# Even and odd heads in one PSUM bank each, first decay products straight from PSUM, three low weight parts on TensorE, and a new order for the first pairs

## The chip, the cores and the metric

The kernel runs on one NeuronCore of a Trainium2 chip. Its time is the device time of one execution in microseconds (us). Engines: TensorE (PE; its weight loads are listed as PEld), VectorE (DVE), ScalarE (ACT), GpSimd (POOL) and SyncE (SP, which issues the DMAs).

## The reference

Three stages follow each other: a linear attention with per-channel decay, a gated expert with RMS norm, and a second expert with squared ReLU. There are 4 batches, 8 heads, 768 steps and 48 channels a head; all in float32.

```python
for t in range(S):                      # _attn_ref, state of 48 x 48 per head
    cur = np.einsum('bhd,bhe->bhde', u[None] * kt, vt)
    y[:, :, t] = np.einsum('bhd,bhde->bhe', rt, state + cur)
    state = wt[:, :, :, None] * state + np.einsum('bhd,bhe->bhde', kt, vt)
# _moe_ref, 3072 tokens x 384, d_ff 1536
xn = x / np.sqrt(np.mean(x * x, -1, keepdims=True) + 1e-06) * rms_g
x = (silu(xn @ w_gate) * (xn @ w_val)) @ w_out
# _moe2_ref, d_ff 2048
r = np.maximum(x @ w_in, 0.0)
out = (s * (r * r) + b) @ w_out
```

## The kernel before

**Tiling.** The 768 steps are cut into 6 chunks of 128. A chunk of one batch is a *pair*, numbered jb = 4 * chunk + batch, so there are 24 (jb0 to jb23). Four pairs make the 512 tokens of one chunk that the first expert reads. The first expert has 12 weight blocks f (gate, value and output part of 128 columns each), the second 16.

**Precision.** Every large product is made of three matmuls: high weight by high input, high by low, low by high. Weights arrive as 64-bit words. DVE puts 32-bit floats together from them in three steps (L585, L589, L591), ACT rounds the high part (L595), DVE takes the low part as a difference (L597).

**One pair of attention** (`attention`, L314). DVE scans the decays forward and backward (L335, L342) and multiplies r and k by them. PE makes the scores in two banks (`scores`, L381) and, in the same step, turns k (L390). ACT copies the two banks to a tiles; POOL zeroes one triangle (`affine_select`, L408). PE then makes in one step (`sums`, L440) the part of the old state (L430), the scores by v (L438) and the new state's product (`news`, L449). DVE adds the two result banks and the diagonal term av to ys, and the state's product to ST. ACT squares ys, POOL takes the root (pow), ACT scales to xg, PE flips xg (`flip`, L547) and ACT and DVE write its high and low part (xh, xl) for the expert. jb0 to jb3 are simpler: no old state, the scores by v in one bank (L447), the mask by DVE, the diagonal through `ac` (L393) and `more` (L465).

**Buffers that tie pairs together.** From jb4 on, three PSUM banks (5, 6, 7) go round: a pair takes two for scores, one for turned k, two for sums, one for the state, one for the flip. IN[q], the tile of r and k, has q = jb % 2, so the r and k of jb10 are loaded once jb8's are used up.

**Order.** Nothing is issued in the order in which it is written. Class `Plan` collects every operation with a priority `when` (smaller goes first), the engines that can do it and a cost for each, and then builds one fixed order per engine: whenever an engine is free it gives it the ready operation of smallest `when`. Until the first product of 512 columns is issued, an idle PE gets *fill* matmuls (L803). The first expert runs in parts: chunk 0 with f 0 to 5, chunk 1 with f 0 to 5 (most of both in 256-token halves), chunk 0 with f 6 to 11, chunk 1 with f 6 to 11, then chunks 2 to 5 with all f. In traces and orders the products into the expert are L623 (w_93 is the gate weight of f 6), those out of it L606 to L608. A weight tile is called by a number, as w_91; tiles of f 10 and 11 are w_1679 to w_1683 in the order of before and w_1586 to w_1591 in that of after.

Of the kernel before, what the change touches and what calls it, by code (L numbers as in the profile page):

```python
# [10 lines left out]
F32 = mybir.dt.float32  # L11
# [12 lines left out]
C = 128  # L24
# [26 lines left out]
TD, LATE = 3, 60  # L51
ORDER = -200, -190, -170, -160, -180, -150
TURNED, EARLY, NU, NM, NZ, LENT = 12, 12, 4, 4, 8, 6

# [45 lines left out]
class Plan:  # L100
# [90 lines left out]
def act(n):  # L191
    return 0.10 + 0.825e-3 * n

# [10 lines left out]
def body(ctx: ExitStack, tc: tile.TileContext, rkw, nat, w1, w2, cst, out):  # L204
# [40 lines left out]
    FL, = tiles(1, "fl", [1, 1], I32)  # L245
    PS = [ps.tile([128, NB], F32, name=f"b{i}") for i in range(8)]
    ident = cs[:, CI:CH]
    mask = MK.rearrange("p (o t) -> p o t", o=1).to_broadcast([128, HP, C])
# [39 lines left out]
    def dma(when, dst, src, nbytes, reads=(), writes=(), land=0.0):  # L288
        op(when, {"sp": max(0.47, nbytes / 350e3 + 0.06)}, lambda e: nc.sync.dma_start(
            out=dst, in_=src), reads, writes, land)  # L290
# [23 lines left out]
    def attention(jb, t):  # L314
        q, b = jb % 2, jb % B
        ke, re, ne = (DVE, DVE, DVE) if jb < EARLY else (BOTH, BOTH, BOTH)
        last = jb >= NJ - B
# [47 lines left out]
        if jb >= NU:  # L365
            tt(td, ne, DM, n[0], n[0], n[1], ALU.mult, (), [nk])
            tt(td, ne, DM, n[0], n[0], cs[:, CU:CEND].rearrange("p (h d) -> p h d", h=H), ALU.mult, ["cu"], [nk])
            op(td, {"dve": vec2(DM)}, lambda e: nc.vector.tensor_reduce(
                AC[q].rearrange("p h o -> p (h o)"), n[0], AX.X, ALU.add), [nk], [("ac", q)], False)
            if jb < NZ:  # L370
                def scaled(e):
                    for h in range(H):
                        nc.scalar.activation(AV[q][:, h], v[:, h], AF.Copy, scale=AC[q][:, h])

                op(td, {"act": 8 * act(D)}, scaled, [("ac", q), ("v", q)], [("av", q)])
            else:
                tt(td, DVE if jb < EARLY else BOTH, DM, AV[q], v, AC[q].to_broadcast([128, H, D]), ALU.mult,
                   [("ac", q), ("v", q)], [("av", q)])

        def scores(e):  # L380
            for h in range(HP):  # L381
                for c0 in (0, 64) if jb >= NM else (0,):
                    cols = slice(c0, c0 + 64 if jb >= NM else C)
                    for p in range(2):
# [28 lines left out]
        if jb < NU:  # L413
            def times(e):
                nc.scalar.activation(AC[q].rearrange("p h o -> p (h o)"), up, AF.Copy)
                for h in range(H):
                    nc.scalar.activation(AV[q][:, h], v[:, h], AF.Copy, scale=AC[q][:, h])

            op(t, {"act": 9 * act(D)}, times, [("ps", i), ("v", q)], [("av", q), ("ac", q)])
        iy = [bank(jb) for _ in range(1 + (jb >= B))]  # L420
        i = iy[0]
        Y = [PS[i][:, 0:DM].rearrange("p (h d) -> p h d", h=H) for i in iy]
# [3 lines left out]
        def quarters(e):  # L426
            for h in range(HP):
                for c0 in (0, 64):
                    for p in range(2):
                        nc.tensor.matmul(Y[p][c0:c0 + 64, 2 * h + p, :], r[64 * p:64 * p + D, h, c0:c0 + 64],  # L430
                                         ST[b][64 * p:64 * p + D, h, p, :], start=h == 0, stop=False,
                                         skip_group_check=True)
# [8 lines left out]
        def sums(e):  # L441
            if jb >= B:
                quarters(e)
            else:
                for j in range(H):
                    p, h = divmod(j, HP)
                    nc.tensor.matmul(Y[0][:, 2 * h + p, :], AT[A[p]][:, h, :], v[:, 2 * h + p, :],  # L447
                                     start=j == 0, stop=j == H - 1, skip_group_check=True)
            if U is not None and jb >= NU:  # L449
                news(e)  # L450
# [18 lines left out]
        reads = [("a", s) for s in A]  # L469
        if jb < NU:  # L470
            op(t, {"pe": 1.8}, sums, reads + [("v", q)], [("ps", i)])
            op(t, {"pe": 0.7}, more, [("av", q), "cs"], [("ps", i)])
            op(t, {"pe": 0.6}, news, [("v", q)] + tk, [("ps", iu)])
            ys, yk = PS[i][:, 0:DM], ("ps", i)
        else:
            op(t, {"pe": 1.5 + 0.6 * (not last)}, sums,
               reads + [("r", q), ("v", q), ("st", b, 0), ("st", b, 1)] + tk * (not last),
               [("ps", i) for i in iy] + ([] if last else [("ps", iu)]))
# [9 lines left out]
        if not last:  # L488
            for p, z in ((0, slice(0, 64)), (1, slice(64, RW))):
                s, pmb = ST[b][z, :, p], PM[q][z].to_broadcast([z.stop - z.start, HP, D])  # L490
                if jb >= B:
                    tt(t, ("dve",), HP * D, s, U[z], s, ALU.add, [("ps", iu)], [("st", b, p)])
                    tt(t, BOTH, HP * D, s, s, pmb, ALU.mult, [("pm", q)], [("st", b, p)])
                else:
# [41 lines left out]
    def hand_over(t):  # L536
        op(t, {"pool": 0.0}, lambda e: None, (), ROOM, False)

    def attention_x(jb, t):
        x, b, z = jb // B % 2, jb % B, jb % 2 if jb < NZ else 0  # L540
# [9 lines left out]

        op(t, {"pe": 0.42}, flip, [("xg", z), "cs"], [("ps", i)])
        sl = slice(b * C, (b + 1) * C)
# [9 lines left out]
    def weights(ph, f, t, slots, clamp=False):  # L562
        src = (w1, w2)[ph]
        for c0, n in ((0, 2), (2, 1))[:2 - ph]:
# [28 lines left out]
            for i in range(n):  # L593
                c, s = slice(i * DM, (i + 1) * DM), slots[c0 + i]
                op(t, {"act": act(DM)}, lambda e, c=c, s=s, pat=pat: nc.scalar.activation(  # L595
                    W[s][:, 0], pat(c).bitcast(F32), AF.Copy), [("pat", pi)], [("wh", s)])
                op(t, {"dve": vec2(DM)} if ph == 0 else {"dve": vec2(DM), "pool": gps(DM)}, lambda e, c=c, s=s, pat=pat: E[e].tensor_tensor(  # L597
                    W[s][:, 1], pat(c).bitcast(F32), W[s][:, 0].bitcast(F32), ALU.subtract),
# [177 lines left out]
    def start():  # L776
# [19 lines left out]

        def empty(e):
            for g in ST:
                nc.gpsimd.memset(g.rearrange("p h j d -> p (h j d)"), 0.0)

        def idle():
# [7 lines left out]

        op(-300, {"dve": 1.9}, consts, (), ["c", "z"])  # L810
        op(-300, {"pool": 1.0}, zeros, (), [("g", 0), ("g", 1)], False)
# [205 lines left out]
```

## Time and profile before

| | us |
|---|---|
| median of 3 runs (lowest, highest) | 984.51 (983.59, 984.66) |
| profiled execution | 986.03 |
| its span | 983.5 |
| PE busy | 962.5 (98%) |
| DVE busy | 661.3 (67%) |
| ACT, POOL busy | 370.9, 174.4 |
| share of PE in the chain that ended last | 84% (DVE 8%, DMA 4%) |

PE is busy nearly throughout, so what PE does not do in time, or does in more time, is the run's time. The first 150 us, in which four pairs are made ready and all weights of the first expert are decoded, differ from the rest: DVE is busy there for 136.7 of 150 us and PE stands still or runs fills in places. The granted TensorE clock is full (2.4 GHz) except at the start and in one place at 100 us.

### The profile page before, as it was taken

Reading aid. Unit: us, or ns where it says so; the run is one execution under the profiler, and the core shown is the slowest. Engines: PE = TensorE matmul, PEld = TensorE weight load, DVE = VectorE, ACT = ScalarE, POOL = GpSimd, SP = SyncE. Lnnn points to the kernel's source line nnn. Section 1 sums busy time; section 2 is a strip of 40 time slices with the busy share of each in tenths; the row PEclk is TensorE's granted clock in tenths of the full one; section 3 lists DMA queues with packets and bytes.
Section 4 is the critical chain, followed back from the end, with each engine's and each line's share of the span. In section 5 each row is a group of like instructions: output and inputs, shape, how many; then the busy total and the mean of one; then the engine's idle time right before and its main releaser. Section 6 shows DMA issues by size and latency. Waiting matters only on the chain.

```text
span 983.5 us, 17703 instructions
## 1 busy us (share of the span) xinstructions
PE 962.5 (98%) x7172; PEld 794.9 (81%) x7174; DVE 661.3 (67%) x1080; ACT 370.9 (38%) x751; POOL 174.4 (18%) x232
## 2 busy tenths in 40 slices
PE   9997999999999999999999999999999999999997
PEld 5886888888878888888888878888888888888886
DVE  7998899556655665543388889986778884433332
ACT  4645553343322422333243344343343433433333
POOL 3203210244424234211005440000000000000000
PEclk9999899999999999999999999999999999999999
DMA  7654463233634543222365565553354430000001
GB/s 249 186 161 135 140 192 112 74 112 87 166 91 97 140 115 81 80 71 70 78 221 188 180 202 183 174 170 97 123 182 157 163 130 1 33 1 1 33 1 36
DMA packets 74426, 115.87 MB, mean 118 GB/s; under 512 B 28384, under 2 KB 48096, under 8 KB 74336
## 3 DMA queue, kind: packets, MB, share of 16 engines
q1 hardware_dynamic: 74336, 114.65, 38.5%
q8 instruction: 58, 0.95, 0.4%
q14 instruction: 32, 0.26, 0.1%
HBM read 99.16 MB, written 15.47 MB: 117 GB/s over the span
## 4 chain that ended last, share of the span: by engine, by line
PE 84%; DVE 8%; DMA 4%; ACT 2%; issue 1%; POOL 1%; SPq 0%; DVEq 0%; POOLq 0%; ACTq 0%
PE b L623 45%; PE b L606 11%; PE b L607 11%; PE b L608 11%; DMA raw<-in_w 2%; PE b L438 2%; PE b L386 2%; DVE pat L589 1%; DVE pat L591 1%; PE b L430 1%; DMA in<-in_rkw 1%; DVE eb L342 1%; DVE w L597 1%; DMA n<-in_nat 1%; DVE pat L585 1%
## 5 line engine op out<-in xcount | busy, mean ns | idle before, releaser
L623 PE MATMUL b<-xh,w 128*128 128x512 f32 (+1 forms) x1566 | 487.2, 376 | 1.0 <-DVE sg L295 0.6
L623 PEld LDWEIGHTS b<-xh,w 128*128 128x128 f32 x1566 | 288.2, 189 | 57.3 <-DVE sg L295 2.1
L623 PE MATMUL b<-xl,w 128*128 128x512 f32 (+1 forms) x783 | 291.9, 373 | 0.0
L606 PE MATMUL b<-hh,w 128*128 128x512 f32 (+1 forms) x537 | 205.4, 382 | 1.3 <-ACT in L658 0.7
L607 PE MATMUL b<-hl,w 128*128 128x512 f32 (+1 forms) x537 | 203.2, 378 | 2.0 <-DVE hl L295 2.0
L608 PE MATMUL b<-hh,w 128*128 128x512 f32 (+1 forms) x537 | 202.5, 377 | 0.0
L298 ACT ACTIVATE sg<-b 128x512 f32<-128x512 f32 (+1 forms) x179 | 102.1, 570 | 244.3 <-PE b L623 238.5
L623 PEld LDWEIGHTS b<-xl,w 128*128 128x128 f32 x783 | 147.9, 189 | 25.2
L694 DVE SCALAR_TENSOR_TENSOR sg<-sg,cs,b 128x512 f32<-128x512 f32 (+1 forms) x97 | 71.8, 740 | 88.3 <-ACT sg L298 88.1
L607 PEld LDWEIGHTS b<-hl,w 128*128 128x128 f32 x537 | 101.4, 189 | 20.9 <-DVE hl L295 2.8
L606 PEld LDWEIGHTS b<-hh,w 128*128 128x128 f32 x537 | 101.4, 189 | 20.9 <-ACT in L658 0.9
L608 PEld LDWEIGHTS b<-hh,w 128*128 128x128 f32 x537 | 101.3, 189 | 18.6
L697 DVE SCALAR_TENSOR_TENSOR hl<-sg,cs,hh 128x512 fp32r<-128x512 f32 (+1 forms) x97 | 73.0, 752 | 45.7 <-ACT hh L298 45.6
L298 ACT ACTIVATE hh<-sg 128x512 fp32r<-128x512 f32 (+1 forms) x82 | 47.4, 578 | 136.9 <-DVE sg L295 136.8
L298 ACT ACTIVATE hh<-sg,cs 128x512 fp32r<-128x512 f32 (+1 forms) x97 | 69.8, 720 | 76.5 <-DVE sg L694 73.2
L295 DVE TENSOR_TENSOR sg<-b,sg 128x512 f32<-128x512 f32 (+1 forms) x82 | 50.8, 620 | 60.7 <-PE b L623 60.2
L295 DVE TENSOR_TENSOR hl<-sg,hh 128x512 fp32r<-128x512 f32 (+1 forms) x82 | 57.8, 704 | 21.6 <-ACT hh L298 21.1
L597 POOL TENSOR_TENSOR w<-pat,w 128x384 fp32r<-128x384 f32 x29 | 39.8, 1391 | 67.6 <-ACT w L595 67.6
L408 POOL TENSOR_SCALAR_AFFINE_SELECT a<-a 128x512 f32<-128x512 f32 x38 | 31.4, 846 | 87.5 <-ACT a L298 87.4
L595 ACT ACTIVATE w<-pat 128x384 fp32r<-128x384 f32 x68 | 32.9, 519 | 32.0 <-DVE pat L591 31.9
L295 DVE TENSOR_TENSOR in<-in,eb 112x512 f32<-112x512 f32 x28 | 20.4, 738 | 24.6 <-DMA in<-in_rkw 24.6
L295 POOL TENSOR_TENSOR st<-st,pm 64x192 f32<-64x192 f32 (+1 forms) x38 | 23.1, 607 | 71.9 <-DVE st L295 52.3
(131 smaller groups left out, 876.0 us busy)
## 6 DMA issues: line engine op xcount, KB each, us to landing
raw<-in_w SPq DMA_DIRECT2D x56, 768.0 KB, 4.3
in<-in_rkw SPq DMA_DIRECT2D x24, 448.0 KB, 4.6
raw<-in_w SPq DMA_DIRECT2D x24, 384.0 KB, 3.3
n<-in_nat SPq DMA_DIRECT2D x18, 384.0 KB, 3.4
in<-in_rkw SPq DMA_DIRECT2D x24, 226.6 KB, 3.1
x2d<-o SPq DMA_DIRECT2D x21, 256.0 KB, 2.8
a<-in_rkw SPq DMA_DIRECT2D x24, 224.0 KB, 3.8
v<-in_nat SPq DMA_DIRECT2D x24, 192.0 KB, 4.0
```

The source lines that it names most:

```text
L295: op(when, {e: cost[e] for e in engines}, lambda e: E[e].tensor_tensor(dst, a, b, f), reads, writes, port)
L298: op(when, {"act": act(n)}, lambda e: nc.scalar.activation(dst, src, func, **kw), reads, writes)
L386: nc.tensor.matmul(sc[p][cols, h, c0:], k[rows, h, cols], r[rows, h, c0:], start=True, stop=True, skip_group_check=True)
L408: op(t, {"pool": 0.60}, lambda e, s=A[p]: nc.gpsimd.affine_select(out=AT[s], in_=AT[s], compare_op=ALU.is_gt, fill=0.0, base=0, pattern=[[ ...
L595: op(t, {"act": act(DM)}, lambda e, c=c, s=s, pat=pat: nc.scalar.activation(W[s][:, 0], pat(c).bitcast(F32), AF.Copy), [("pat", pi)], [("w ...
L597: op(t, {"dve": vec2(DM)} if ph == 0 else {"dve": vec2(DM), "pool": gps(DM)}, lambda e, c=c, s=s, pat=pat: E[e].tensor_tensor(W[s][:, 1], ...
L606: nc.tensor.matmul(dst, wt[:, 0, cols], xh, start=first, stop=False, skip_group_check=True)
L607: nc.tensor.matmul(dst, wt[:, 0, cols], xl, start=False, stop=False, skip_group_check=True)
L608: nc.tensor.matmul(dst, wt[:, 1, cols], xh, start=False, stop=last, skip_group_check=True)
L623: nc.tensor.matmul(dst, W[s][:, w, kk * 128:(kk + 1) * 128], xx[x][:, kk, sl], start=first and j == kk == 0, stop=last and kk == KD - 1 an ...
L694: op(t, {"dve": vec2(n)}, lambda e: nc.vector.scalar_tensor_tensor(sg, sg, s_col, p, ALU.mult, ALU.mult), [("ps", i)], [("sg", q)], False)
L697: op(t, {"dve": vec2(n)}, lambda e: nc.vector.scalar_tensor_tensor(hl, sg, b_col, hh.bitcast(F32), ALU.add, ALU.subtract), [("sg", q), ("h ...
```

## The change

- **Sums by head parity.** In `attention` the scores by v use all 128 rows at once: even heads are summed in one bank and odd heads in the other, 16 products of 128 rows by 64 columns in place of 32 of 64 by 64. The two DVE additions that follow take 192 columns each (before: 384 each). The state tile loses its dimension of parity, so its addition and its decay product are one operation of 112 partitions each, not two.
- **First decay products.** For jb0 to jb3, DVE multiplies the new state in PSUM by the decay at once; before, ACT copied it in two operations and DVE or POOL multiplied the copies later. POOL no longer clears ST at the start.
- **Low parts on PE.** For f 0, the three low weight parts are made on PE: identity by float minus identity by high part, in bank 1; ACT copies the result.
- **Diagonal term.** av comes from ACT in four operations of two heads for all jb below 12 (before: ACT below 8, DVE for 8 to 11).
- **Order.** A table FIRST_OPS replaces the priority of about 130 of the first 812 operations, and some costs in the planner are new. The table is cut to two lines here. Operations 747, 751 and 761 in it are a scan, a product and the scores of jb8.

```diff
+FIRST_OPS = {
...
+    511: -263.4, 548: 827.8, 549: 709, 552: 454, 556: 831.9, 590: 439.1, 592: 673.5, 596: 450.7, 605: 467.4,
...
+    685: -155.7, 688: 8.6, 747: 1340.2, 751: 1405.6, 754: 1892.3, 755: -1192.9, 756: -460, 761: 834.5, 800: -206.5,
...
+}
+ONPE = 1
...
-        self.ops.append((when, engines, fn, port))
+        self.ops.append((FIRST_OPS.get(i, when), engines, fn, port))
...
 def act(n):
-    return 0.10 + 0.825e-3 * n
+    return 0.19 + 0.65e-3 * n
...
-    ST = tiles(B, "st", [RW, HP, 2, D])
+    ST = tiles(B, "st", [RW, HP, D])
...
-            if jb < NZ:
-                def scaled(e):
...
-                op(td, {"act": 8 * act(D)}, scaled, [("ac", q), ("v", q)], [("av", q)])
+            if jb < EARLY:
+                scale_v(td, q, v)
             else:
-                tt(td, DVE if jb < EARLY else BOTH, DM, AV[q], v, AC[q].to_broadcast([128, H, D]), ALU.mult,
-                   [("ac", q), ("v", q)], [("av", q)])
+                tt(td, BOTH, DM, AV[q], v, AC[q].to_broadcast([128, H, D]), ALU.mult,
+                   [("ac", q), ("v", q)], AVK)
...
-                        nc.tensor.matmul(Y[p][c0:c0 + 64, 2 * h + p, :], r[64 * p:64 * p + D, h, c0:c0 + 64],
-                                         ST[b][64 * p:64 * p + D, h, p, :], start=h == 0, stop=False,
...
+                        rows = slice(64 * p, 64 * p + D)
+                        nc.tensor.matmul(Y[p][c0:c0 + 64, 2 * h + p, :], r[rows, h, c0:c0 + 64], ST[b][rows, h, :],
+                                         start=h == 0, stop=False, skip_group_check=True)
...
             for j in range(H):
                 h, p = divmod(j, 2)
                 for c0 in (0, 64):
-                    for z in range(2):
-                        rows = slice(64 * z, 64 * z + 64)
-                        nc.tensor.matmul(Y[z][c0:c0 + 64, j, :], AT[A[p]][rows, h, c0:c0 + 64], v[rows, j, :],
-                                         start=False, stop=j == H - 1, skip_group_check=True)
...
+                    nc.tensor.matmul(Y[p][c0:c0 + 64, j, :], AT[A[p]][:, h, c0:c0 + 64], v[:, j, :],
+                                     start=jb < B and j == 0, stop=j >= H - 2, skip_group_check=True)
...
-            tt(t, DVE, DM, ys, PS[iy[0]][:, 0:DM], AV[q].rearrange("p h d -> p (h d)"), ALU.add,
-               [("ps", iy[0]), ("av", q)], [yk])
-            tt(t, DVE, DM, ys, PS[iy[1]][:, 0:DM], ys, ALU.add, [("ps", iy[1])], [yk])
+            for p in range(2):
+                y2, a2, s2 = [x.rearrange("p (h j d) -> p h j d", h=HP, j=2)[:, :, p] for x in (
+                    PS[iy[p]][:, 0:DM], AV[q].rearrange("p h d -> p (h d)"), ys)]
+                tt(t, DVE, HP * D, s2, y2, a2, ALU.add, [("ps", iy[p])] + AVK, [yk])
...
-                if jb >= B:
-                    tt(t, ("dve",), HP * D, s, U[z], s, ALU.add, [("ps", iu)], [("st", b, p)])
-                    tt(t, BOTH, HP * D, s, s, pmb, ALU.mult, [("pm", q)], [("st", b, p)])
-                else:
-                    cp(t, HP * D, s, U[z], [("ps", iu)], [("st", b, p)])
-                    tt(t + LATE, BOTH, HP * D, s, s, pmb, ALU.mult, [("pm", q)], [("st", b, p)])
+            if jb >= B:
+                tt(t, DVE, HP * D, st, U, st, ALU.add, [("ps", iu)], [("st", b)])
+                tt(t, BOTH, HP * D, st, st, pmb, ALU.mult, [("pm", q)], [("st", b)])
+            else:
+                tt(t, DVE, HP * D, st, U, pmb, ALU.mult, [("ps", iu), ("pm", q)], [("st", b)])
...
+    def scale_v(t, q, v):
+        for h0 in range(0, H, 2):
+            def run(e, h0=h0):
+                for h in (h0, h0 + 1):
+                    nc.scalar.activation(AV[q][:, h], v[:, h], AF.Copy, scale=AC[q][:, h])
+
+            op(t, {"act": 2 * act(D)}, run, [("ac", q), ("v", q)], [("av", q, h0)])
...
+                on_pe = ph == 0 and f < ONPE and not clamp
...
+                        nc.tensor.matmul(PS[1][:, 0:DM], ident, pat(c).bitcast(F32), start=True, stop=False, skip_group_check=True)
+                        nc.tensor.matmul(PS[1][:, 0:DM], minus, W[s][:, 0], start=False, stop=True, skip_group_check=True)
...
-        op(-199, {"pool": 1.6}, empty, (), [("st", b, p) for b in range(B) for p in range(2)], False)
```

What the new priorities do to the order is seen at three places. The first is DVE where chunk 1 comes to the end of its products with f 0 to 5; sg_121 in the 256-column row is the gated product of f 5, whose value weight is w_91 (in_128 and in_129 are the r and k tiles of even and odd pairs, eb and rg belong to the decay scans). Before:

```order
L597 TENSOR_TENSOR w_1681<-pat_114,w_1681 128x384
L589 SCALAR_TENSOR_TENSOR pat_113<-raw_111,pat_113 128x768
L335 SCALAR_TENSOR_TENSOR eb_133<-in_129,ones_68 112x516
L591 SCALAR_TENSOR_TENSOR pat_113<-raw_111,pat_113 128x768
L295 TENSOR_TENSOR sg_121<-b_157,sg_121 128x256
L340 RECIPROCAL rg_70<-eb_133 112x4x8
L597 TENSOR_TENSOR w_1680<-pat_113,w_1680 128x384
```

And after:

```order
L603 SCALAR_TENSOR_TENSOR pat_113<-raw_111,pat_113 128x768
L314 TENSOR_TENSOR hl_124<-sg_120,hh_122 128x256
L314 TENSOR_TENSOR sg_121<-b_157,sg_121 128x256
L362 SCALAR_TENSOR_TENSOR eb_134<-in_128,rg_69 112x516
L618 TENSOR_TENSOR w_103<-pat_113,w_103 128x384
L618 TENSOR_TENSOR w_101<-pat_114,w_101 128x384
L618 TENSOR_TENSOR w_102<-pat_113,w_102 128x384
```

The gated product of w_91 stands 16 rows earlier on DVE (row 237, before 253); weights of f 8 to 10 that preceded it now follow it.

The second place is PE from the sums of one pair to the scores of the next, among chunk 2's pairs (a is the score tile, kt the turned k, xg the normed result; b_156 to b_163 are the PSUM banks). Before, with jb9 and jb10:

```order
L438 MATMUL b_161<-v_131,a_137 64x48
L462 MATMUL b_162<-v_131,kt_135 64x48
L462 MATMUL b_162<-v_131,kt_135 48x48
L623 MATMUL b_156<-xh_117,w_96 128x512
L606 MATMUL b_158<-hh_122,w_95 128x512
L607 MATMUL b_158<-hl_124,w_95 128x512
L549 MATMUL b_163<-cs_63,xg_139 128x128 x3
L623 MATMUL b_157<-xh_117,w_97 128x512
L386 MATMUL b_161<-in_128 64x128
```

After, from the last product of chunk 1 (w_1587) through jb8 to jb9:

```order
L644 MATMUL b_157<-xh_117,w_1587 128x512
L402 MATMUL b_162<-in_128 64x128
L406 MATMUL b_161<-cs_63,in_128 128x112 x4
L443 MATMUL b_162<-st_71,in_128 64x48
L452 MATMUL b_162<-v_130,a_137 64x48 x2
L452 MATMUL b_163<-v_130,a_138 64x48 x2
L467 MATMUL b_161<-v_130,kt_135 64x48
L561 MATMUL b_162<-cs_63,xg_139 128x128 x3
L402 MATMUL b_163<-in_129 64x128
```

Rows of the same kind between those shown are left out. In the order of before, 18 expert matmuls of 512 columns stand between jb9's sums and its flip, and 9 more between the flip and jb10's scores; in that of after no expert matmul stands between jb8's scores and the end of jb11's sums. All of jb8 to jb11 comes there as one block, behind chunk 1's last product and ahead of chunk 2's first.

The third place is ACT in that block. Before, around the scores of jb9 (a_136 and a_137 are the copies of its scores):

```order
L298 ACTIVATE xh_116<-b_162,cs_63 128x128 x3
L298 ACTIVATE hh_123<-sg_121 128x512
L298 ACTIVATE sg_120<-b_156 128x512
L298 ACTIVATE a_136<-b_163 128x512
L298 ACTIVATE a_137<-b_161 128x512
```

After, for jb9 as well:

```order
L317 ACTIVATE xg_139<-ys_142,rs_148 128x384
L317 ACTIVATE xh_116<-b_162,cs_63 128x128 x3
L547 ACTIVATE av_140<-v_130,ac_146 128x48 x8
L317 ACTIVATE a_136<-b_163 128x512
L317 ACTIVATE a_137<-b_161 128x512
```

The eight operations for av_140 belong to jb10 and now stand ahead of jb9's score copies; for jb11's av and jb10's copies it is the same.

## Rows read from the trace of the kernel before

**Rows 1.** Page, part 1: busy us, share of the span, instructions.

```profile
PE 962.5 (98%) x7172; PEld 794.9 (81%) x7174; DVE 661.3 (67%) x1080; ACT 370.9 (38%) x751; POOL 174.4 (18%) x232
```

**Rows 2.** Stretches: length, busy (count) of PE, PEld, DVE, ACT, POOL; clock, DMA, GB/s.

```profile
0.00:150.00 150.00, 138.00 (x1528) 117.46 (x1530) 136.67 (x260) 78.86 (x230) 35.68 (x62) 0.98 0.58 179
150.00:242.00 92.00, 92.00 (x953) 75.95 (x952) 60.91 (x108) 33.63 (x73) 28.82 (x43) 1.00 0.33 92
90.00:100.00 10.00, 4.99 (x151) 3.77 (x150) 9.04 (x16) 5.13 (x17) 3.71 (x7) 0.97 0.56 155
100.00:110.00 10.00, 9.62 (x144) 8.62 (x144) 9.31 (x16) 5.25 (x16) 2.20 (x3) 0.69 0.34 87
```

**Rows 3.** DVE and ACT groups to 250 us: count, busy, mean ns, idle before.

```profile
L557 DVE SCALAR_TENSOR_TENSOR xl<-b,cs,xh 128x128 fp32r<-128x128 f32 x36 | 10.4, 343 | 8.6 <-ACT xh L298 8.6
...
L373 ACT ACTIVATE av<-v,ac 128x48 f32<-128x48 f32 x32 | 7.6, 321 | 1.4 <-DVE ac L368 1.3
```

**Rows 4.** PE in order, 10 to 24 us: start, duration, instruction, count.

```profile
11.63 1.88 PE L447 MATMUL b<-v,a 128*128 128x48 f32 x16
13.44 0.67 PE L462 MATMUL b<-v,kt 128*64 128x48 f32 x16
14.03 0.91 PE L466 MATMUL b<-av,cs 128*128 128x384 f32 x2
```

**Rows 5.** PE and DVE in order at 154 us.

```profile
153.33 1.23 DVE L335 TENSOR_TENSOR_SCAN eb<-in,ones 112x516 f32<-112x516 f32 x1
...
154.08 0.28 PE L623 MATMUL b<-xl,w 128*128 128x256 f32 x1
...
154.20 0.52 PE L623 MATMUL b<-xh,w 128*128 128x256 f32 x2
...
155.32 0.42 DVE L295 TENSOR_TENSOR sg<-b,sg 128x256 f32<-128x256 f32 x1
```

**Rows 6.** PE in order at 245 us.

```profile
246.32 0.50 PE L623 MATMUL b<-xh,w 128*128 128x512 f32 x1
```

**Rows 7.** All engines in order, 180 to 187 us, pair jb8.

```profile
180.04 0.68 PE L430 MATMUL b<-st,in 48*64 48x48 f32 x32
...
180.55 1.11 PE L438 MATMUL b<-v,a 64*64 64x48 f32 x64
180.79 0.33 SPq L289 DMA_DIRECT2D in<-in_rkw  x1
...
181.59 0.67 PE L462 MATMUL b<-v,kt 128*64 128x48 f32 x16
...
182.59 0.54 DVE L295 TENSOR_TENSOR ys<-b,ys 128x384 f32<-128x384 f32 x1
...
183.16 0.53 ACT L298 ACTIVATE xg<-ys 128x384 f32<-128x384 f32 x1 [2.35 <-DVE ys L295]
...
185.01 0.62 ACT L298 ACTIVATE xg<-ys,rs 128x384 f32<-128x384 f32 x1 [0.91 <-POOL rs L486]
...
185.65 1.29 DVE L295 TENSOR_TENSOR in<-in,eb 112x512 f32<-112x512 f32 x2 [2.14 <-DMA in<-in_rkw]
...
186.44 0.49 PE L549 MATMUL b<-cs,xg 128*128 128x128 f32 x3
```

**Rows 8.** All engines in order from 195 us, pair jb9.

```profile
195.08 1.10 PE L386 MATMUL b<-in 48*64 48x128 f32 x32
...
196.11 0.60 PE L390 MATMUL b<-cs,in 112*128 112x112 f32 x4
196.24 1.09 ACT L298 ACTIVATE a<-b 128x512 f32<-128x512 f32 x2 [0.40 <-PE b L386]
...
196.91 1.22 POOL L408 TENSOR_SCALAR_AFFINE_SELECT a<-a 128x512 f32<-128x512 f32 x2 [0.54 <-ACT a L298]
```

**Rows 9.** PE in order, 94 to 98 us.

```profile
94.03 0.39 PE L608 MATMUL b<-hh,w 128*128 128x512 f32 x1
97.95 0.55 PE L549 MATMUL b<-cs,l 128*128 128x128 f32 x3 [3.53 <-DMA n<-in_nat]
```

More of the change, by code (lines that the diff above doesn't have):

```diff
@@ L246, in body @@
     PS = [ps.tile([128, NB], F32, name=f"b{i}") for i in range(8)]
+    minus = sb.tile([128, 128], F32R, name="minus")
     ident = cs[:, CI:CH]
@@ L315, in attention @@
         q, b = jb % 2, jb % B
+        AVK = [("av", q, h0) for h0 in range(0, H, 2)]
         ke, re, ne = (DVE, DVE, DVE) if jb < EARLY else (BOTH, BOTH, BOTH)
@@ L369, in attention @@
                 AC[q].rearrange("p h o -> p (h o)"), n[0], AX.X, ALU.add), [nk], [("ac", q)], False)
-            if jb < NZ:
-                def scaled(e):
-                    for h in range(H):
-                        nc.scalar.activation(AV[q][:, h], v[:, h], AF.Copy, scale=AC[q][:, h])
-                op(td, {"act": 8 * act(D)}, scaled, [("ac", q), ("v", q)], [("av", q)])
-            else:
-                tt(td, DVE if jb < EARLY else BOTH, DM, AV[q], v, AC[q].to_broadcast([128, H, D]), ALU.mult,
-                   [("ac", q), ("v", q)], [("av", q)])
+            if jb < EARLY:
+                scale_v(td, q, v)
+            else:
+                tt(td, BOTH, DM, AV[q], v, AC[q].to_broadcast([128, H, D]), ALU.mult,
+                   [("ac", q), ("v", q)], AVK)
         def scores(e):
             for h in range(HP):
-                for c0 in (0, 64) if jb >= NM else (0,):
-                    cols = slice(c0, c0 + 64 if jb >= NM else C)
+                for c0 in (0, 64) if jb >= B else (0,):
+                    cols = slice(c0, c0 + 64 if jb >= B else C)
                     for p in range(2):
@@ L413, in attention, with state @@
         if jb < NU:
[L414 to L419, printed above, removed]
+            cp(t, H, AC[q].rearrange("p h o -> p (h o)"), up, [("ps", i)], [("ac", q)])
+            scale_v(t, q, v)
         iy = [bank(jb) for _ in range(1 + (jb >= B))]
         i = iy[0]
-        Y = [PS[i][:, 0:DM].rearrange("p (h d) -> p h d", h=H) for i in iy]
+        Y = [PS[i][:, 0:DM].rearrange("p (h d) -> p h d", h=H) for i in (iy * 2)[:2]]
         iu = None if last else bank(jb)
         U = None if last else PS[iu][:RW, 0:HP * D].rearrange("p (h d) -> p h d", h=HP)
-        def quarters(e):
+        def state(e):
             for h in range(HP):
@@ L429, in quarters, with sums @@
                     for p in range(2):
-                        nc.tensor.matmul(Y[p][c0:c0 + 64, 2 * h + p, :], r[64 * p:64 * p + D, h, c0:c0 + 64],
-                                         ST[b][64 * p:64 * p + D, h, p, :], start=h == 0, stop=False,
-                                         skip_group_check=True)
+                        rows = slice(64 * p, 64 * p + D)
+                        nc.tensor.matmul(Y[p][c0:c0 + 64, 2 * h + p, :], r[rows, h, c0:c0 + 64], ST[b][rows, h, :],
+                                         start=h == 0, stop=False, skip_group_check=True)
+        def sums(e):
+            if jb >= B:
+                state(e)
             for j in range(H):
@@ L435, in quarters @@
                 for c0 in (0, 64):
-                    for z in range(2):
-                        rows = slice(64 * z, 64 * z + 64)
-                        nc.tensor.matmul(Y[z][c0:c0 + 64, j, :], AT[A[p]][rows, h, c0:c0 + 64], v[rows, j, :],
-                                         start=False, stop=j == H - 1, skip_group_check=True)
-        def sums(e):
-            if jb >= B:
-                quarters(e)
-            else:
[L445 to L449, printed above, removed]
+                    nc.tensor.matmul(Y[p][c0:c0 + 64, j, :], AT[A[p]][:, h, c0:c0 + 64], v[:, j, :],
+                                     start=jb < B and j == 0, stop=j >= H - 2, skip_group_check=True)
+            if U is not None and jb >= B:
                 news(e)
@@ L469, in attention @@
         reads = [("a", s) for s in A]
-        if jb < NU:
-            op(t, {"pe": 1.8}, sums, reads + [("v", q)], [("ps", i)])
-            op(t, {"pe": 0.7}, more, [("av", q), "cs"], [("ps", i)])
+        if jb < B:
+            op(t, {"pe": 1.0}, sums, reads + [("v", q)], [("ps", i)])
+            op(t, {"pe": 0.7}, more, AVK + ["cs"], [("ps", i)])
             op(t, {"pe": 0.6}, news, [("v", q)] + tk, [("ps", iu)])
@@ L488, in attention @@
         if not last:
-            for p, z in ((0, slice(0, 64)), (1, slice(64, RW))):
-                s, pmb = ST[b][z, :, p], PM[q][z].to_broadcast([z.stop - z.start, HP, D])
-                if jb >= B:
-                    tt(t, ("dve",), HP * D, s, U[z], s, ALU.add, [("ps", iu)], [("st", b, p)])
-                    tt(t, BOTH, HP * D, s, s, pmb, ALU.mult, [("pm", q)], [("st", b, p)])
-                else:
-                    cp(t, HP * D, s, U[z], [("ps", iu)], [("st", b, p)])
-                    tt(t + LATE, BOTH, HP * D, s, s, pmb, ALU.mult, [("pm", q)], [("st", b, p)])
+            st, pmb = ST[b], PM[q].to_broadcast([RW, HP, D])
+            if jb >= B:
+                tt(t, DVE, HP * D, st, U, st, ALU.add, [("ps", iu)], [("st", b)])
+                tt(t, BOTH, HP * D, st, st, pmb, ALU.mult, [("pm", q)], [("st", b)])
+            else:
+                tt(t, DVE, HP * D, st, U, pmb, ALU.mult, [("ps", iu), ("pm", q)], [("st", b)])
         cp(t, DM + 170, xg, ys, [yk, ("rs", q)], [xk], scale=rs[:, 0:1])
@@ L549, in flip @@
                 nc.tensor.transpose(xtp[:, kk, :], XG[z][:, kk * 128:(kk + 1) * 128], ident)
-        op(t, {"pe": 0.42}, flip, [("xg", z), "cs"], [("ps", i)])
+        op(t, {"pe": 0.26}, flip, [("xg", z), "cs"], [("ps", i)])
         sl = slice(b * C, (b + 1) * C)
@@ L795, in masks @@
                                     channel_multiplier=-1)
-        def empty(e):
-            for g in ST:
-                nc.gpsimd.memset(g.rearrange("p h j d -> p (h j d)"), 0.0)
         def idle():
```

10 lines of the change are left out of this document (8 added, 2 removed), and 13 rows, old and new, of the table FIRST_OPS.

## The prediction, made before the changed kernel was run

> **What bounds the kernel now.** I read the page's busy times first: PE is busy for 962.5 of 983.5 us [rows 1], so a gain must come out of the 21 us in which PE stands still, its fills, or less PE work, and any new PE wait goes onto the time in full. The stretches then say where that is. To 150 us PE is idle for 12.0 us and DVE busy for 136.7 us, idle for 13.3; from 150 to 242 us PE is busy for all of 92.0 us while DVE works for 60.9 [rows 2]. The first 150 us are DVE's, what follows is PE's. So I read the order of PE and DVE at the seam (154 us), the course of one pair where PE never waits for it (jb8 and jb9), and the one place where PE does wait for a pair (94 to 98 us).
>
> Chunk 0's second half, first product w_93, begins at 154.3 us in the middle of a row of two records [rows 5]. Chunk 2's first product follows jb12's sums at 246.32 [rows 6]. From there on PE runs to the end in both orders with the same expert work, so the sum is made at that point and carried to the end.
>
> **Early part: gain.** DVE reaches the gated product of w_91 (row 253 of its order) at 155.32 us [rows 5]. In the new order that is row 237. Counting both lists up to it, with each instruction's distance from start to start: 22 weight instructions fewer (10 low parts, three of them by PE, and 12 decode steps; most come later, where DVE has 31 us to spare [rows 2]), 11.5 us; sums and states 2.1 less, since an addition of 192 columns replaces one of 384; products of n and av 1.9 less; scans and products by decays 4.0 more, as jb9's come earlier. That is 11.5 less in all, so DVE can be there at 143.8. In before PE had ended w_91's product 1.0 earlier and went straight to w_93. Now 18 matmuls of 256 columns come between, 0.12 us from start to start [rows 5], 2.2 us, so w_93 starts at 145.0 if DVE idles as before. The new order makes the four first pairs before any expert product, and jb4's scores come right behind, which takes away waits: of DVE's 13.3 idle us I count 3 as saved. w_93 starts at 142.0, rounded with the rest to a gain of 12. Bounds: 8 (no idle saved, PE 1 us late); and 21, if all 12.0 idle us of PE go, the 3 us of its low clock (below), and 6 us with the 15 fills fewer that the new order has (62, not 77).
>
> The low parts on PE are six matmuls of 384 columns, in all some 3 us, and stand among the fills before the first expert product; they cost nothing unless DVE, freed of them, makes PE wait there. POOL's clearing of ST and ACT's copies of the first states were beside other work and give nothing by themselves.
>
> **Sums by parity: PE.** In before 64 records took 1.04 us (180.55 to 181.59 [rows 7]). Now there are 32 of 128 rows by 64 columns. The nearest row is the state's product, the same rows and columns, alternating between the array's column halves as the new sums do: 16 records from 13.44 with 0.67 us to the end of the last, about 0.60 of them before the next can start [rows 4, 7]; twice 0.60 is 1.20, a loss of 0.16 a pair, 2.6 us for the 16 pairs behind w_93. The other end is the 16 records of 128 by 128, 1.81 us (11.63 to 13.44 [rows 4]), as 32 halves again 1.81: a loss of 0.77 a pair, 12.3. The lower end is no loss. I take 2.6, by the row of the same shape.
>
> **The block of jb8 to jb11: loss.** In before nine to eighteen expert matmuls of 512 columns stand in every gap of a pair; in the new order nothing does, from jb8's scores to jb11's sums, and each pair's scores stand behind the flip of the pair before. PE has to sit out what the rows show.
>
> - Scores to sums. Scores start at 195.08; turned k follows at 196.11; ACT's two copies start at 196.24; POOL's second triangle ends at 196.91 + 1.22 = 198.13 [rows 8]: 3.05 us. PE has scores (1.03), turned k (0.4) and the state part (180.04 to 180.55, 0.51 [rows 7]) to do, 1.9. It waits 1.1.
> - Sums to flip. From 180.55 to the end of the second ys is 2.58, then from 183.16 the square, the root and xg run to 185.01 + 0.62 = 185.63, 2.5 [rows 7]. The smaller additions save about 0.4. With 0.1 to the flip that is 4.8; PE has sums and state product, 1.2 + 0.6. It waits 3.0. In before the flip came at 186.44 behind expert work and nobody waited.
> - That happens in full for jb8, jb9 and jb10; jb11's flip lies behind expert products, so it has the first wait alone: 3 x 4.1 + 1.1 = 13.4 us.
> - ACT's order. jb9's score copies now stand behind eight av operations of jb10 (7.6 us for 32, so 1.9 [rows 3]). These wait for DVE, which comes to the sum for them only after jb8's three xl (0.87 [rows 3]), a scan (1.23 [rows 5]) and the sum itself (0.54, as an operation of that size [rows 7]). From the flip of jb8: 0.3 + 0.9 + 1.2 + 0.5 + 1.9 = 4.8, where the copies would else start 0.3 + 1.2 after it: 3.3 more. On DVE the product of jb10's r stands ahead of this too. Its load is issued 0.75 after the state part and ends 4.86 later (180.79 to 185.65 [rows 7]); with the product (1.29) it is done before jb8's flip, so it adds nothing. The same for jb10's copies behind jb11's av: 6.6 in all.
>
> The block's waits are 13.4 to 20.0 us; I take the middle, 17, because DVE may be ahead with a part of what jb10's and jb11's av wait for; the first end has no such wait at all, the second has it twice in full. jb8's scores and turned k, which stood ahead of w_93, are now behind it: 1.4 more. jb12's sums are now ahead of chunk 2's first product, as in before.
>
> **The clock.** PE was idle for 3.5 us before the flip at 97.95 [rows 9] and busy for 4.99 of the 10 us around; in the next 10 us the granted clock was 0.69 of full, so part of them ran at 1.2 instead of 2.4 GHz, which cost 3.1 us [rows 2]. The block has about 24 us of work in 41 or more, nearly as bad. I count one such fall, 3.1. Bounds: nothing, and 11 if the three pairs from jb9 on (3.7 of PE work each) run at half the clock.
>
> **Sum.** -12.0 + 2.6 + 17.0 + 1.4 + 3.1 = +12.1. The profiled execution took 986.03; 998.1 in its terms. It lay 1.5 above the median of the runs, so I expect 996.6.
>
> **Rivals.**
> - *Faster: the early gain outweighs the block.* For it: PE's idle time and fills before 150 us are large, and the new order gives the early pairs to PE while it would only fill. Against: DVE is busy for 91% there, and its saved work is 11.5 us only to that point. With 21 early, no loss in the sums, the block at 13.4 and no fall of the clock: -21 + 1.4 + 13.4 = -6.2, 978.3. It decides from an early gain of 16 on, if the block costs its least.
> - *No change.* The same with a gain near 15: 984.
> - *The clock stays low through the block.* For it: the waits return every 4 us. Against: at 90 to 100 us the clock was still 0.97 in the stretch of the wait itself [rows 2]. 11 in place of 3.1: 1004.5.
> - *Full-height sums run as slow as the 128 by 128 ones.* 12.3 in place of 2.6: 1006.3. Against it stands the state's row at 0.60 for 16; for it, that row has 48 columns in half of its loads. The Trainium skill has a rule on its side: by "TensorE: Matmul & The Clock Gate", Part 3, a weight load overlaps matmuls in flight only where its group of rows differs, and the new sums use every row each time. By that rule the state's product, full height too, could not start a record every 0.04 us; the trace shows that it does, so I give it little.
> - *The early gain is small,* because the new order makes DVE wait for weights that it asks for earlier: 4 in place of 12, 1004.6.
>
> **How the numbers follow.** Forecast 0.55, its own range 988 to 1004. Faster rival 0.14, no change 0.05, low clock 0.12, slow sums 0.07, small early gain 0.07. A measurement of this kernel can tell 0.2% (2 us) from nothing. The slower cases add up to 0.81. The range goes from the faster rival's time to well above the slow ones, as two of these may meet: 979 to 1010.
>
> **What would show it.** In the changed profile: w_93's first product near 142 us (133 to 146); then an unbroken PE to about 214; then some 42 us in which PE is half idle, with its flips waiting for ACT's xg and its sums for POOL's triangles, about 3 and 1 us each; ACT's av ahead of the score copies; a granted clock under 0.8 in or behind the block; the sums at 1.2 us a pair; chunk 2's first product near 256 (before 246.32), and from there to the end 2 us more than before. It is wrong if the block's waits come to less than 10 us, or if chunk 2's first product starts before 246.

## The result, and the profile after

The changed kernel takes 997.97 us (median of 4, 997.14 to 1002.02), the kernel before 984.59 in the same series; the ratio of the mean times is 1.0139, 95% interval 1.0104 to 1.0174. It is slower, near the forecast of 996.6 and inside the range. The profiled execution took 997.48, span 995.7.

The page, parts 1 and 2 of the changed kernel (against [rows 1]; a digit is a fortieth of the span):

```profile
PE 966.8 (97%) x6585; PEld 799.5 (80%) x6589; DVE 638.2 (64%) x1052; ACT 378.0 (38%) x782; POOL 158.3 (16%) x210
...
PE   9999999977899999999999999999999999999997
...
PEclk9999999975999999999999999999999999999999
```

The loss is in one place: digits 9 and 10 (200 to 250 us) are the only ones in which PE and its clock are low together. Stretches of the changed kernel, columns as in [rows 2]:

```profile
0.00:131.90 131.90, 128.40 (x1438) 111.72 (x1443) 125.09 (x247) 74.63 (x222) 22.33 (x49) 1.00 0.63 188
150.00:205.00 55.00, 54.85 (x256) 44.80 (x256) 19.49 (x33) 14.22 (x24) 2.03 (x2) 1.00 0.09 29
204.67:257.91 53.24, 37.51 (x607) 30.35 (x606) 27.32 (x49) 21.63 (x61) 25.52 (x38) 0.67 0.41 113
```

Up to 205 us PE hardly ever stands still. Then come 53.2 us in which it is busy for 37.5, at 0.67 of its clock. What stands at the ends of the first and last of these stretches and between them, in the order of PE and DVE (against [rows 5, 6]; the first stretch is cut 0.2 us behind the start of its instruction): w_91's gated product on DVE, w_93's first product, jb8's scores, chunk 2's first product.

```profile
131.72 0.42 DVE L314 TENSOR_TENSOR sg<-b,sg 128x256 f32<-128x256 f32 x1
...
133.61 0.40 PE L644 MATMUL b<-xh,w 128*128 128x512 f32 x1
...
204.67 1.10 PE L402 MATMUL b<-in 48*64 48x128 f32 x32
...
257.91 0.80 PE L644 MATMUL b<-xh,w 128*128 128x512 f32 x1
```

w_93 comes 20.7 us earlier than before (154.31 to 133.61), chunk 2's first product 11.6 later (246.32 to 257.91). From there to the end it is 0.6 more (737.8 against 737.2). That is the whole difference of the spans, 12.2.

Inside the block, jb8 to jb9 and on to jb10 (against [rows 7, 8]):

```profile
207.84 1.25 PE L452 MATMUL b<-v,a 128*64 128x48 f32 x32
208.91 0.63 PE L467 MATMUL b<-v,kt 128*64 128x48 f32 x16
...
212.59 0.55 PE L561 MATMUL b<-cs,xg 128*128 128x128 f32 x3 [3.05 <-ACT xg L317]
213.07 1.97 PE L402 MATMUL b<-in 48*64 48x128 f32 x32
...
213.94 1.90 ACT L547 ACTIVATE av<-v,ac 128x48 f32<-128x48 f32 x8
...
215.74 1.07 ACT L317 ACTIVATE a<-b 128x512 f32<-128x512 f32 x2
...
216.38 1.58 PE L443 MATMUL b<-st,in 48*64 48x48 f32 x32 [0.35 <-ACT a L317]
...
224.83 0.90 PE L561 MATMUL b<-cs,xg 128*128 128x128 f32 x3 [3.62 <-ACT xg L317]
225.66 1.97 PE L402 MATMUL b<-in 48*64 48x128 f32 x32
```

The flips wait 3.05 and 3.62 us for xg, as forecast. After the first such wait the clock is at half: scores take 1.97 instead of 1.10. From scores to scores it is 8.4 us for jb8, 12.6 for jb9 (12.8 for jb10). At full clock the new sums take 1.07 (207.84 to 208.91), practically the 1.04 of before.

PE's waits of the changed kernel to 300 us, the largest (total, times, longest):

```profile
PE b L561 <- ACT xg L317: 9.9, 3, 3.6
PE b L443 <- DVE xl L569: 3.0, 1, 3.0
```

### The profile page after: what moved, and what is told of

It is laid out like the page before. It is cut to its first block, busy times and chain, and to the rows that moved or that the text cites. A ratio compares the mean times of both kernels' runs of the same rounds, so it can differ in the third digit from the quotient of the medians.

```text
span 995.7 us, 16531 instructions
## 1 busy us (share of the span) xinstructions
PE 966.8 (97%) x6585; PEld 799.5 (80%) x6589; DVE 638.2 (64%) x1052; ACT 378.0 (38%) x782; POOL 158.3 (16%) x210
## 4 chain that ended last, share of the span: by engine, by line
PE 75%; DVE 4%; DMA 4%; ACT 2%; POOL 1%; issue 1%; SPq 0%; DVEq 0%; POOLq 0%; ACTq 0%
PE b L644 40%; PE b L627 10%; PE b L628 10%; PE b L629 10%; DMA in<-in_rkw 2%; PE b L452 2%; DMA raw<-in_w 2%; PE b L402 1%; PE b L443 1%; DVE pat L603 1%; DVE pat L601 1%; POOL a L424 1%; SPq L308 0%; DVE hl L314 0%; DVE pat L597 0%
## 5 line engine op out<-in xcount | busy, mean ns | idle before, releaser
L314 DVE TENSOR_TENSOR ys<-b,av 128x192 f32<-128x192 f32 x40 | 13.8, 351 | 41.4 <-PE b L452 41.4
L603 DVE SCALAR_TENSOR_TENSOR pat<-raw,pat 128x768 uint32<-128x768 uint32 (+1 forms) x40 | 35.2, 879 | 0.0
```

What stands on the lines that cost most here:

```text
L314: op(when, {e: cost[e] for e in engines}, lambda e: E[e].tensor_tensor(dst, a, b, f), reads, writes, port)
L603: op(t, {"dve": vec2(N)}, lambda e, word=word, pat=pat: nc.vector.scalar_tensor_tensor(pat(), word(0), 29, pat(), ALU.logical_shift_right, ...
```

## The experiments

Ratios are of mean times, to the kernel before in the same series, with the 95% interval.

**Taking one number out.** Edit of the changed kernel:

```diff
-    685: -155.7, 688: 8.6, 747: 1340.2, 751: 1405.6, 754: 1892.3, 755: -1192.9, 756: -460, 761: 834.5, 800: -206.5,
+    685: -155.7, 688: 8.6, 747: 1340.2, 751: 1405.6, 754: 1892.3, 755: -1192.9, 756: -460, 800: -206.5,
```

> One entry of the table is taken out, 761: 834.5, so that jb8's scores get the priority they had in before; everything else is the changed kernel. Theory A (the block costs some 30 us and nothing else was lost): the pairs jb8 to jb11 lie between expert products again, PE does not wait in 200 to 260 us, the clock stays at 1.0 there, the early lead of 20.7 us of the changed kernel stays, chunk 2's first product starts near 228 us and the time is about 967 us. Rival B (the early lead is borrowed: DVE work for these pairs was only put off, and comes back as waits between 135 and 230 us): the time is 978 to 985. Rival C (the new shape of the sums or the low parts on PE cost the time): the time stays above 990.

969.95 us, ratio 0.9857 (0.9831 to 0.9884): 28 us less than the changed kernel, and with one variant of it below the fastest kernel here. Its stretches from 150 us, and chunk 2's first product:

```profile
150.00:180.00 30.00, 29.95 (x161) 24.02 (x160) 21.88 (x40) 15.97 (x46) 2.71 (x3) 1.00 0.27 82
180.00:210.00 30.00, 30.00 (x335) 24.39 (x335) 18.11 (x32) 14.46 (x37) 13.19 (x20) 1.00 0.36 108
210.00:240.00 30.00, 29.43 (x297) 23.82 (x296) 18.73 (x30) 11.55 (x26) 14.98 (x22) 1.00 0.58 143
```

```profile
230.12 0.39 PE L644 MATMUL b<-xh,w 128*128 128x512 f32 x1
```

PE is full and at full clock where the block was; chunk 2 begins at 230.1, 27.8 us earlier. Theory A holds, 3 us short of its number. w_93 starts at 139.37 here, 14.9 us ahead of the kernel before and not 20.7: jb8's scores (130.18) and sums stand ahead of it here, so a part of the 20.7 was work put off behind w_93. At chunk 2's first product 16.2 us of lead are left. So B falls but for these few us, and C falls: the time is far below 990 with the new sums and low parts in place.

**No table at all.** `FIRST_OPS = {}`.

> The table of priorities is empty; the operations and the planner's costs are those of the changed kernel. If the early lead comes from the order of the table (theory A), w_93 starts near 148 us, from the 4 us of DVE work that the sums, states and low parts save and a few more, and the time is about 979. If it comes from the operations themselves (rival), w_93 starts near 136 and the time is about 968, like that of the run with only one entry taken out. If the operations are worth nothing, 984.

982.19, ratio 0.9970 (0.9944 to 0.9995). w_93 starts at 154.97, no earlier than before (I had expected 148). So the new operations and costs are worth 0.5 to 5.5 us together by the interval, and the early lead needs the table. The table with the old operations was not tried.

**The one number alone.** `FIRST_OPS = {761: 834.5}`.

> The empty table with the one entry 761: 834.5 put back. In the built order jb8's scores stand behind the first product of chunk 1's second half, not in a block. Theory Q (a late priority only holds an operation back where PE always has something else ready; without the other entries PE runs dry at times and takes it): time as without a table, 979 to 985, and no stretch from 200 to 260 us with a low clock. Rival (the number is harmful by itself): above 995.

982.23, ratio 0.9967 (0.9943 to 0.9991), as without a table; jb8's scores start at 136.46, the clock is at 1.00 from 200 to 260 us. Theory Q holds, and its reason can be followed in `Plan`, which computes the order from the kernel's source alone. In this plan jb8's scores are ready by 125.9 us of the planner's time and taken at 129.1, when PE's list holds nothing else. In the plan of the changed kernel they are ready by 118.5, and something of a smaller number is in the list each time until 202.4. The rest of the table makes such a plan.

**The four late numbers of jb8 out.** As the first run, and 747, 751 and 754 removed too.

> The changed kernel without the four late entries of jb8 (747, 751, 754, 761: scan, product of r, product of n, scores). Theory A: the block is gone as with the one entry out, time 968 to 972; the three others only shift DVE work that has room, so no difference to that run. Rival: with jb8's DVE work earlier the early lead shrinks, 974 to 980.

979.30, ratio 0.9934 (0.9901 to 0.9966): 9 us slower than with 761 alone out. The rival holds. w_93 starts at 149.80 instead of 139.37, and PE waits again for the kinds of tiles that it waited for in the kernel before:

```profile
PE b L561 <- ACT xg L317: 2.5, 1, 2.5
PE b L402 <- DVE in L314: 1.9, 1, 1.9
PE b L406 <- DVE xl L569: 1.7, 2, 1.1
```

The three late numbers of jb8's scan and products on DVE are thus good for 10 us in this table; of the four only that of the scores on PE is harmful. Whether the 10 us come from this DVE work itself or from a plan that falls out differently, no run separates.

**Low parts, twice.** On DVE, with the plan made anew from that cost:

```diff
-                    op(t, {"pe": 0.85}, low, [("pat", pi), ("wh", s), "cs", "minus"], [("ps", 1)])
-                    cp(t, DM, W[s][:, 1], PS[1][:, 0:DM], [("ps", 1)], [("wl", s)])
+                    op(t, {"dve": vec2(DM)}, lambda e, c=c, s=s, pat=pat: nc.vector.tensor_tensor(
+                        W[s][:, 1], pat(c).bitcast(F32), W[s][:, 0].bitcast(F32), ALU.subtract),
+                       [("pat", pi), ("wh", s)], [("wl", s)])
+                    op(t, {"pool": 0.0}, lambda e: None, (), (), False)
```

> As the run with only entry 761 taken out, and the three low weight parts of f 0 made by DVE as in before (an empty operation keeps the numbering of the table). Theory A: PE did these parts where it would only fill, so their price on DVE decides: w_93 starts 1 to 2 us later than in that run and the time is 1 to 2 us longer. Rival: PE's 3 us of these parts were on the path, and the time is 1 to 3 us shorter.

979.98, ratio 0.9959 (0.9941 to 0.9976), 10 us slower, which neither theory had. Then on DVE with the plan kept, so that only the instruction changes its engine:

```diff
-                        nc.tensor.matmul(PS[1][:, 0:DM], ident, pat(c).bitcast(F32), start=True, stop=False, skip_group_check=True)
-                        nc.tensor.matmul(PS[1][:, 0:DM], minus, W[s][:, 0], start=False, stop=True, skip_group_check=True)
+                        nc.vector.tensor_tensor(W[s][:, 1], pat(c).bitcast(F32), W[s][:, 0].bitcast(F32), ALU.subtract)
```

> As the run with only entry 761 taken out, and the three low parts made by DVE, but in the plan of that run: every other instruction stays in its order (in the run with low parts on DVE and a plan made anew the time was 10 us longer). Theory A (the 10 us came from the plan that fell out differently, not from the operation): time 970 to 973, w_93 within 2 us of 139.4. Rival B (DVE's 1.4 us more ahead of the first expert products shift everything behind): time 976 to 981, w_93 near 146 to 152.

970.45, ratio 0.9846 (0.9804 to 0.9887), w_93 at 141.0: as the first run. The 10 us were the plan that fell out differently; the operation itself is worth nothing that can be measured, whichever engine makes it.

**What sets the block's length.** Six runs, all with the block. First fills for the clock, four in `sums` behind the state part and twelve in `flip`, each 512 columns of zeros into bank 1:

```diff
+            if 2 * B <= jb < 3 * B:
+                fills(4)
...
+            if 2 * B <= jb < 3 * B - 1:
+                fills(12)
```

> The changed kernel with its block, and with 4 fill matmuls of 512 columns on zeros ahead of the score sums of jb8 to jb11 and 12 ahead of the flips of jb8 to jb10, 0.9 and 2.6 us at full clock, where PE stands still for 0.2 to 1.1 and 3.0 to 3.6 us. Theory A1 (about half of the block's 30 us is the low clock): the clock stays at 1.0 or nearly so, a pair's scores take 1.0 us again instead of 1.97, chunk 2's first product starts 10 to 13 us earlier (near 246) and the time is about 986. Rival A2 (the block's length is set by the waits on ACT, POOL and DVE alone, the slow matmuls lie beside them): the clock comes back and the time stays at 996 to 1000.

1000.16, ratio 1.0166 (1.0117 to 1.0215). Scores took 1.10 again, yet chunk 2 began at 261.3. The four fills ahead of the sums lay on the path themselves: without them it began at 258.6.

> The changed kernel with its block and 12 fill matmuls of 512 columns on zeros ahead of the flips of jb8 to jb10 only, where PE stood still 3.0 to 3.6 us; none ahead of the score sums, where the run with 16 fills a pair put up to 1.9 us on the path. Theory O (the slow clock and ACT's order hide each other: ACT is busy with av while PE's slow scores run): the clock rises to about 0.9, a pair takes 12 us instead of 12.7, chunk 2's first product comes 0 to 4 us earlier than 257.9, the time is 994 to 998. Rival A1 (the clock alone accounts for half of the block's loss): a pair takes 9 us, chunk 2's first product near 247, time near 987.

996.61, ratio 1.0114 (1.0065 to 1.0162). A pair still took 12.5 to 13.4. But this run does not take the clock away as a cause. The granted clock was 0.84 over the block, against 0.67, and 0.50 again from 218 to 224 and from 232 to 238 us, in the sums and in the fills themselves. The fills took 3.8 and 4.0 us there, 2.8 ahead of jb8's flip, and held up two flips: xg was there at 225.05 and 238.18, the flips start at 225.92 and 239.28.

```profile
224.44 0.61 ACT L317 ACTIVATE xg<-ys,rs 128x384 f32<-128x384 f32 x1 [0.66 <-POOL rs L492]
...
225.92 0.49 PE L567 MATMUL b<-cs,xg 128*128 128x128 f32 x3
```

Then av of jb8 to jb11 in one DVE multiplication, without fills and with them:

```diff
+                if dve:
+                    if h0 == 0:
+                        nc.vector.tensor_tensor(AV[q], v, AC[q].to_broadcast([128, H, D]), ALU.mult)
+                    return
```

> The changed kernel with its block; av of jb8 to jb11 is one multiplication on DVE in the place where ACT's eight operations stood, all else in the same order. Theory O: at the slow clock the score copies only wait 0.6 us for ACT, so the block shortens by 1 to 2 us, time near 996. My forecast's term (3.3 us for each of two pairs): 6 to 7 us shorter, time near 991.

> Both edits of the two runs before: fills ahead of the flips and av on DVE. Theory O: together they take away more than the sum of the two apart, some 8 us, time near 989, a pair in 10 us. Rival A1: the same as with the fills alone. If a pair still takes over 12 us, the block's length is set by the other waits (xl ahead of turned k, the copies ahead of the state part) and neither the clock nor ACT's order matters.

996.74, ratio 1.0131 (1.0079 to 1.0183), and 996.38, ratio 1.0109 (1.0063 to 1.0155). The times of the single edits lie where theory O had them, though the block is no shorter (chunk 2 begins at 258.6 and 258.2); its 8 us for both together did not come, nor A1's 10, nor the 6 to 7 of my forecast's term for ACT. Then, on top of both edits, POOL's two memsets to DVE, and last the flips to bank 0 as well:

```diff
+        op(t - 15, {"pool": 0.5}, lambda e: nc.vector.memset(IN[q][96:128, OK:], 0.0), (), [("k", q)], False)
...
+        op(t, {"pool": 0.08}, lambda e: (nc.vector if 2 * B <= jb < 3 * B + 2 else nc.gpsimd).memset(
...
+        xtp = PS[0 if 2 * B <= jb < 3 * B - 1 else i][:, 0:DM].rearrange("p (k t) -> p k t", k=KD)
```

> As the run with fills ahead of the flips and av on DVE, and POOL's two memsets of the block (which wait for the next pair's scan on DVE and stand ahead of the score triangles) issued on DVE instead. In that run PE waited 4.4 us for triangles in the block, up to 2.4 at one pair, and a pair took 11.7 us. Theory P (several chains of nearly the same length run side by side in the block: flip, xl, scan, memset, triangle is the next one behind the clock and ACT): the waits for triangles fall to 1 to 2 us in all and the time falls by 2 to 4 us to about 993. Rival: another chain of the same length is left (turned k behind xl, the load of r and k) and the time stays at 995 to 997.

> As the run with fills, av on DVE and POOL's memsets on DVE, and the flips of jb8 to jb10 go to bank 0 instead of the next bank of the ring, so that the next pair's turned k no longer waits until xl has left the flip's bank (4.0 us of PE waits in the block of that run, 1.3 a pair). Theory R (with clock, ACT and POOL out of the way, that wait is on the loop from flip to flip): a pair takes 10.5 to 11 us instead of 12, the block is 3 to 4 us shorter, time 992 to 994. Rival: the loop from xg through flip to xl and the load of r and k hold it at 12 us, time 995 to 998.

997.23, ratio 1.0132 (1.0103 to 1.0161), and 999.26, ratio 1.0153 (1.0136 to 1.0170). Neither P's 2 to 4 us nor R's 3 to 4 came, and the last time lies above the range of R's rival too. None of the six beats the changed kernel by more than these series can tell. The last run's trace (of its fastest execution, 995.20) shows one reason. Rows of all engines from jb8's flip to jb9's:

```profile
213.00 0.55 PE L571 MATMUL b<-cs,xg 128*128 128x128 f32 x3 [0.35 <-ACT xg L317]
...
215.75 1.27 DVE L355 TENSOR_TENSOR_SCAN eb<-in,ones 112x516 f32<-112x516 f32 x1
216.95 0.52 DVE L388 TENSOR_REDUCE ac<-n 128x8 f32<-128x384 f32 x1
...
217.54 0.33 SPq L308 DMA_DIRECT2D n<-in_nat  x1
...
220.68 0.99 POOL L314 TENSOR_TENSOR n<-n 128x384 f32<-128x384 f32 x1 [3.23 <-DMA n<-in_nat]
...
223.45 0.55 POOL L492 TENSOR_TENSOR rs<-rs,col 128x1 f32<-128x1 f32 x1
224.03 0.61 ACT L317 ACTIVATE xg<-ys,rs 128x384 f32<-128x384 f32 x1 [2.69 <-POOL rs L492]
224.70 0.55 PE L571 MATMUL b<-cs,xg 128*128 128x128 f32 x3 [1.43 <-ACT xg L317]
```

Here is a loop of 11.7 us that has little of PE in it: flip, xh and xl, the next scan on DVE, the sum over n that sets the tile n free, the load of a later pair's n (3.1 us from issue), POOL's products on it, and behind them on POOL the root that xg and so the next flip wait for. In the next round the load took 5.4 us (229.32 to 234.72) and the round 14.4:

```profile
229.32 0.35 SPq L308 DMA_DIRECT2D n<-in_nat  x1
...
234.72 0.99 POOL L314 TENSOR_TENSOR n<-n 128x384 f32<-128x384 f32 x1 [5.49 <-DMA n<-in_nat]
...
238.39 0.61 ACT L317 ACTIVATE xg<-ys,rs 128x384 f32<-128x384 f32 x1 [5.14 <-POOL rs L492]
```

In the changed kernel the load is issued at the same place (POOL waited 1.16 us for it at 219.73) and ends beside PE's slow matmuls; there, and with fills ahead of the flips alone, POOL's root for jb9 and jb10 waits for ACT and not for this load. Taking away one of two chains of equal length gains nothing. The last three runs also put av (0.55 us), and two of them the memsets, on DVE, that is on this loop. Moving the load or POOL's products was not tried, so that this loop holds the block once the others are gone is read from the trace, not shown.

## Why the prediction came out right, point by point

- **Where and which way: right.** The block at the place in the order that was foretold (from 205 us, foretold 214, by the error in the early part), its waits on xg (9.9 us for three flips, forecast 9.0), the start of chunk 2 at 257.9 (forecast 256), the same distance to the end. The one-number run shows that the block costs 28 us.
- **Early part: the term was too small,** 20.7 in place of 12 (14.9 with the one number out), at its bound of 21. Up to w_91's gated product DVE was busy for 125.1 us in 131.9. Before, it was so for 141.9 in 155.3; the stretch of before:

```profile
0.00:155.32 155.32, 143.31 (x1568) 122.61 (x1571) 141.89 (x268) 80.19 (x233) 36.39 (x64) 0.98 0.57 176
```

  That is 17 less work where I had counted 11.5, and 6.8 us idle instead of 13.4, where I had counted on 3 saved. Of the 5 us more, about 3 are that instructions of the same form were shorter on balance (the decode steps of 384 columns at L585, now L597, last 351 ns on the mean against 422); why, I did not test, and POOL was busy for 22.3 us in that time, against 36.4. The other 2 are the 22 weight instructions, 13.9 us by their mean durations before, where I counted 11.5. The run with four numbers out shows that 10 us hang on the three late numbers of jb8's DVE work, for which my sum had no term of its own. The run without a table shows that the operations and costs alone bring w_93 no nearer; my 2.1 and 1.9 us for them are not seen there.
- **The block: too small as well,** and that hid the first error. From w_93 to chunk 2's first product it was 124.3 us against 92.0, 32.3 more; I had 17.0 + 3.1 + 1.4 and 0.6 for four sums, 22. In its stretch of 53.2 us PE stood still for 15.7, near my waits of 17.0. It was busy for 37.5, where I had counted some 24 us of work, so by this account the excess lies in slow matmuls.
- **The waits: right in sum, in part by luck.** The flips' are right. For POOL's triangles PE waited 1.2 us in three pairs, forecast 1.1 in each of four; for ACT's copies it waited 1.3 us in all, where ACT's order alone was to cost 6.6 at most and 3.6 in the sum; 3.0 came that I had not foreseen (below).
- **ACT's order: wrong.** The av operations needed no later scan: in the trace they start at 213.94, before the scan (214.88), and the copies come 0.6 us late, not 3.3. I had taken the sum behind the scan for theirs; it belongs to the pair after.
- **The clock: mis-sized.** 0.67 over 53 us, not one fall of 3.1 us. This is the term that was too small. What full clock would give back stays open: the fills raised it to 0.84 only and held up flips themselves, and in the last run, where jb9's scores (1.10) and sums ran at full speed in the first round shown, the loop through DVE, the load of n and POOL still took 11.7 us, against 12.2 from flip to flip in the changed kernel (212.59 to 224.83).
- **A wait not foreseen:** 3.0 us at the end of the block, before jb12's state part, for xl, which stands behind a product on DVE that waited for the load of r and k.
- **Sums by parity:** 0.03 us a pair instead of 0.16. The rival with the slow sums is out: full-height records followed each other every 0.033 us, their weight loads beside them. The rule of the Trainium skill ("TensorE: Matmul & The Clock Gate", Part 3), by which a weight load overlaps matmuls in flight only where its group of rows differs, is not borne out by this trace.

So that the number came so near is luck: two errors of 9 and 10 us of opposite sign. The place and the mechanism, one block in which PE waits at a low clock and loses more than the early part gains, were right by themselves; of its parts ACT's order was wrong and the clock's share far too small.

## What to carry to other kernels

A priority is worth what the ready queue makes of it: the same late number did nothing in a plan where the engine runs dry, and cost 28 us in one where it did not run dry for the next 84 us of the planner's time. Read the built order for stretches in which one engine's work stands without its usual company, and look at every step of the loop around it before pricing one; if two loops have the same length, removing either shows nothing. Before reading a probe that fills idle time, see that it does not end later than what was waited for. To price an operation, keep the order and change only the engine that does it; a new plan moves more than the operation.

## What was not expected of the hardware

The granted clock stayed at 0.50 for 20 us in which PE was busy for 60% of the time. Rows of the changed kernel:

```profile
220.00:230.00 10.00, 6.00 (x85) 4.62 (x85) 5.49 (x12) 5.59 (x18) 4.58 (x8) 0.50 0.25 78
230.00:240.00 10.00, 5.99 (x105) 5.17 (x97) 2.95 (x8) 2.41 (x7) 7.04 (x9) 0.50 0.46 130
```
